# Scratch matmuls in several tilings, and scratch operations on VectorE and Pool, behind the last results of an attention and MLP mix

## The chip, the cores and the metric

The kernel runs on one core of a Trainium2 chip. The metric is the device time of one execution in microseconds; lower is better. The time of the kernel before is the median of two runs on the chip.

The engines are named as the profile names them: PE is TensorE (PEld its weight loads), DVE is VectorE, ACT is ScalarE, POOL is GpSimd, SP is SyncE, which here only issues transfers.

## The reference

From one input `x` (2048 rows of 512) the kernel computes attention with 32 heads that share one key and one value of width 16, computes an MLP with a squared ReLU from another weight set and input, and mixes the two by a gate per row:

```python
g = _sigmoid((x * gate_w).sum(-1, keepdims=True))
a = _A_ref(x, A_wq, A_wk, A_wv, A_wo)      # softmax(q k^T / 4) v, then @ wo
b = _B_ref(x, B_w1, B_b1, B_w2, B_b2)      # relu(x w1 + b1)^2 @ w2 + b2
return g * a + (1 - g) * b
```

All inputs and the output are float32.

## The kernel before, in words

All work is in `mix_kernel`, with an order written out by hand: the program order is the order on every engine's queue, and the tile framework adds only the waits. Attention is cut into 32 steps (`NC * NG`: 4 chunks of 512 rows, 8 groups of 4 heads), each of 16 key tiles in two halves of 256 rows. `scores` (line 723) multiplies 49 augmented rows of queries and keys, two matmuls on the two halves of the array's rows (line 730), and ScalarE takes the exponential of 1024 columns at a time (line 734). `context` (line 737) multiplies the exponentials by the values: plain float32 matmuls of 128 rows by 32 columns, four heads side by side in the array (line 745, `tile_position=(0, h * 32)`).

The projections and the MLP run as a stream of matmuls of 64 rows by 128 columns in float32r, alternating between the two halves of the rows (`stream`, line 188; the matmul is line 214). Operands are split into a rounded part and a rest (`split`, lines 177 to 179), so that three products give the accuracy of float32. `phase` (line 1003) interleaves the two kinds of work, `plan` decides how much of the stream goes between scores, and small jobs for VectorE wait in lists (`chores`, `side`).

The end is what matters here. After the last attention step, `half(acc, 1)` (line 818) transposes, divides and splits the last 256 rows, with a few matmuls on `junk` between (`busy`, line 851) and the flag `bad` computed on VectorE (line 845): 1 if some softmax denominator left the safe range. Then the loop of lines 1068 to 1074 makes the last two output tiles: three full float32r matmuls each (`mm`, line 186), one VectorE operation that gates and adds (line 1073), and a transfer to `out`, the first issued by SP, the second by ACT.

Behind that every engine loads the flag (line 1076) and branches (line 1077): if it is 1, `exact_shift` recomputes the attention; with these inputs it is skipped. The instructions of the closing barrier carry line 1106, where the context ends.

Tiles come from pools with a fixed number of buffers. `at` holds the exponentials as tiles named `e` (128 x 4 x 512, four buffers), `sp` holds the scores as tiles `s` in PSUM (128 x 2 x 512, two buffers), `mp` the stream's PSUM tiles. A tile that takes a used buffer waits for the buffer's last readers.

Of the kernel before, what the change touches and what calls it, by code (L numbers as in the profile page):

```python
# [10 lines left out]
F32 = mybir.dt.float32  # L11
F32R = mybir.dt.float32r
BF = mybir.dt.bfloat16
I32 = mybir.dt.int32
AF = mybir.ActivationFunctionType
OP = mybir.AluOpType
# [6 lines left out]
NC, CH = 4, 512  # L23
# [126 lines left out]
def mix_kernel(ctx: ExitStack, tc: tile.TileContext, xT, wkv, wq, wo, w12, b1, b2, cst, out):  # L150
    nc = tc.nc
# [101 lines left out]
    with fast, tc.tile_pool(name="at", bufs=1) as at, \  # L253
# [790 lines left out]
        while us:  # L1044
            it, k = divmod(us[0], 2 * NK)
# [22 lines left out]
        for j in range(2, 4):  # L1068
# [3 lines left out]
            s = 4 * (NC - 1) + j  # L1072
            nc.vector.scalar_tensor_tensor(ot, po, g[:, s:s + 1], most[0][:, j], op0=OP.mult, op1=OP.add)  # L1073
            (nc.sync, nc.scalar)[j % 2].dma_start(out[s * 128:(s + 1) * 128], ot)

    flag = nc.values_load(bad[0:1, 0:1], min_val=0, max_val=1)
    with tc.If(flag > 0):
        exact_shift(tc, k_aug, v_ext, qs, oTs, gms, ress, cs, wo, split, outproj, stream, unpack)
# [31 lines left out]
```

## Time and profile before

| what | us |
|---|---|
| runs | 1246.99 and 1248.84 |
| median | 1247.91 |
| span of the profiled execution, first to last instruction | 1243.9 |
| PE busy | 1233.2 (99%) |
| ACT busy | 1060.3 (85%) |
| DVE busy | 623.1 (50%) |
| POOL busy | 59.4 (5%) |
| last matmul begins | 1237.33 |
| last VectorE operations begin | 1237.08 |
| last transfer issued | 1238.55 |

The profile is of one execution. The device time of a run holds the span and what lies around it; the median is 4.0 us over the span. In a row of the timeline the first number is the start from the span's start, the second the length, then engine, line, operation, output and inputs, shapes, and how many instructions were merged. In a row of groups the two numbers behind the bar are the busy time in us and the mean of one in ns. In an answer on one line of the code, a row has the operation, its count, and its shortest, median and longest duration in ns, then the first and the last start in us. A matmul of plain float32 leaves two records, one of float32r leaves one; PE's record of a matmul is longer than the distance to the next, since matmuls are pipelined.

### The profile page before, as it was taken

The numbers are of one execution on the slowest core, as the hardware profiler recorded it, in microseconds if no ns is written. First come the engines' busy times: TensorE is split into PE (matmuls) and PEld (weight loads), VectorE is DVE, ScalarE is ACT, GpSimd is POOL, SyncE is SP. The second block draws the span as 40 slices with busy tenths as digits, with TensorE's granted clock in tenths as the row PEclk, the third lists the DMA queues.
The fourth block names the chain that finished last, engine by engine and source line by source line (L and its number), as shares of the span: only waits on it lengthen the run. The fifth ranks groups of instructions, "written<-read, shape, count | busy, mean of one in ns | idle before, by whom it ended". The sixth has DMA issues, their size and how long they took to land.

```text
span 1243.9 us, 24095 instructions
## 1 busy us (share of the span) xinstructions
PE 1233.2 (99%) x9839; PEld 612.5 (49%) x9839; DVE 623.1 (50%) x1246; ACT 1060.3 (85%) x1178; POOL 59.4 (5%) x75
## 2 busy tenths in 40 slices
PE   9999999999999999999999999999999999999997
PEld 4555555555555555555555555555433333343343
DVE  5666665545565542744827365355441454232433
ACT  6888888888888987988988888888899999999985
POOL 1000300000002000000200000002000000000000
PEclk9999999999999999999999999999999999999999
DMA  6334321211232210222202121121110120011101
GB/s 215 101 96 143 105 79 40 82 48 65 69 113 84 75 57 25 82 73 98 72 29 82 65 81 61 56 81 65 56 57 26 35 69 31 31 48 47 44 31 37
DMA packets 44388, 85.57 MB, mean 69 GB/s; under 512 B 10450, under 2 KB 10706, under 8 KB 43760
## 3 DMA queue, kind: packets, MB, share of 16 engines
q1 hardware_dynamic: 37024, 68.27, 17.0%
q0 software_dynamic: 7104, 15.44, 3.7%
q8 instruction: 79, 1.29, 0.4%
q14 instruction: 37, 0.30, 0.1%
q10 hardware_dynamic: 144, 0.26, 0.1%
HBM read 54.68 MB, written 20.97 MB: 61 GB/s over the span
## 4 chain that ended last, share of the span: by engine, by line
PE 96%; ACT 1%; DVE 1%; DMA 0%; issue 0%; SPq 0%; ACTq 0%
PE acc L745 38%; PE mm L214 31%; PE s L730 25%; ACT e L734 1%; PE mm L312 1%; DMA xf<-in_xT 0%; PE mm L186 0%; PE s L322 0%; DVE kmx L334 0%; PE acc L352 0%; ACT w1r L491 0%; PE mm L802 0%; DVE ot L1073 0%; DVE xlagain L179 0%; DVE w1l L487 0%
## 5 line engine op out<-in xcount | busy, mean ns | idle before, releaser
L734 ACT ACTIVATE e<-s 128x1024 f32<-128x1024 f32 x1024 | 980.3, 1023 | 153.5 <-PE s L730 152.0
L745 PE MATMUL acc<-e,v_ext 128*32 128x512 f32 (+1 forms) x4224 | 509.4, 587 | 0.0
L730 PE MATMUL s<-qa,k_aug 49*128 49x512 f32 x2048 | 452.6, 433 | 0.1
L730 PEld LDWEIGHTS s<-qa,k_aug 49*128 49x128 f32 x2048 | 193.7, 183 | 331.8 <-ACT e L734 300.2
L664 DVE SCALAR_TENSOR_TENSOR res<-mm,omg,res 128x512 f32<-128x512 f32 x128 | 95.8, 750 | 252.2 <-PE mm L214 252.2
L214 PE MATMUL mm<-w2r,hr 64*128 64x512 f32 x896 | 212.2, 393 | 1.0 <-DVE big L641 0.6
L745 PEld LDWEIGHTS acc<-e,v_ext 128*32 128x32 f32 x4224 | 102.7, 108 | 208.7 <-issue 202.0
L214 PE MATMUL mm<-w2l,hr 64*128 64x512 f32 x448 | 159.4, 393 | 0.0
L214 PEld LDWEIGHTS mm<-w2r,hr 64*128 64x128 f32 x896 | 129.0, 187 | 18.4 <-DVE res L664 1.2
L214 PEld LDWEIGHTS mm<-w2l,hr 64*128 64x128 f32 x448 | 83.4, 187 | 7.4
L214 PE MATMUL mm<-xragain,w1l 64*128 64x512 f32 x224 | 80.3, 393 | 0.0
L214 PE MATMUL mm<-xr,w1l 64*128 64x512 f32 x224 | 79.4, 393 | 0.0
L214 PE MATMUL mm<-xlagain,w1r 64*128 64x512 f32 x224 | 79.2, 392 | 0.0
L214 PE MATMUL mm<-xragain,w1r 64*128 64x512 f32 x224 | 78.7, 392 | 0.0
L214 PE MATMUL mm<-xl,w1r 64*128 64x512 f32 x224 | 78.5, 391 | 0.0
L214 PE MATMUL mm<-xr,w1r 64*128 64x512 f32 x224 | 77.0, 392 | 0.0
L641 DVE TENSOR_TENSOR big<-big,mm 128x512 f32<-128x512 f32 x56 | 38.5, 687 | 75.0 <-PE mm L214 74.9
L758 DVE RECIPROCAL n<-n 128x86 f32<-128x86 f32 x90 | 61.9, 688 | 3.1
L637 DVE TENSOR_SCALAR big<-mm,b1t 128x512 f32<-128x512 f32 x56 | 42.0, 750 | 39.0 <-PE mm L214 36.9
L214 PEld LDWEIGHTS mm<-xr,w1r 64*128 64x128 f32 x224 | 41.7, 186 | 4.1
L214 PEld LDWEIGHTS mm<-xragain,w1l 64*128 64x128 f32 x224 | 41.7, 186 | 3.9
L214 PEld LDWEIGHTS mm<-xl,w1r 64*128 64x128 f32 x224 | 41.7, 186 | 3.9
(160 smaller groups left out, 1136.8 us busy)
## 6 DMA issues: line engine op xcount, KB each, us to landing
stage<-in_w SPq DMA_DIRECT2D x56, 256.0 KB
qa<-qs SPq DMA_DIRECT2D x186, 64.0 KB
w1f<-in_w SPq DMA_DIRECT2D x28, 256.0 KB
w2f<-in_w SPq DMA_DIRECT2D x28, 256.0 KB
qs<-qr SPq DMA_DIRECT2D x16, 256.0 KB
ress<-res POOLq DMA_DIRECT2D x4, 1024.0 KB, 4.1
qs<-ql POOLq DMA_DIRECT2D x15, 256.0 KB, 8.2
oc<-accs SPq DMA_DIRECT2D x30, 128.0 KB
```

The costliest lines, as they stand in the source:

```text
L214: nc.tensor.matmul(banks[half], a[rows], b[rows], start=i == 0, stop=i == len(terms) - 1)
L312: nc.tensor.matmul(kvq[c][64 * i:64 * i + 64], wkvf[:, k], xf[c, k], start=a == 0, stop=a == 1, skip_group_check=True, tile_position=(0, 6 ...
L637: nc.vector.tensor_scalar(h[0], p, b1t[:, f:f + 1], None, op0=OP.add)
L641: nc.vector.tensor_tensor(h[0], h[0], p, OP.add)
L664: nc.vector.scalar_tensor_tensor(part, p, omg[:, s:s + 1], part, op0=OP.mult, op1=OP.add)
L730: nc.tensor.matmul(s[:, r].rearrange("p (a n) -> p a n", a=2), k_aug[rows, kt * 128:(kt + 1) * 128], qa[it][rows, :, cols], start=True, st ...
L734: nc.scalar.activation(es[u // 2][:, :, mine], s.rearrange("p r (a n) -> p (r a) n", a=2), AF.Exp, scale=SCALE)
L745: nc.tensor.matmul(acc[h * 32:(h + 1) * 32, cols], v_ext[:, kt], es[u // 2][:, h % 2 * 2 + h // 2, mine], start=(kt == 0), stop=(kt == NK ...
L758: nc.vector.reciprocal(n, n)
```

## The change

Behind the loop that makes the last two output tiles, and still inside the pools, the change allocates three tiles `e` and fills them with 0.5 on VectorE, takes two PSUM tiles `s`, and issues matmuls whose results nobody reads. `pairs_of` issues 8 pairs on the two halves of the rows with 128 and then 96 columns; `full` uses the whole array; `half_pairs` and `sub` use tiles of 64 x 128, and of 64 x 32 and 128 x 32 in plain float32. The four loops alternate between tilings. All matmuls have 512 moving columns. After them stand, in program order, operations of 128 x 1024 elements on VectorE (a bit mask, subtractions, copies) and on Pool (copies, subtractions) between the tiles `e`; nobody reads their results either. Output and flag are computed as before. Line numbers below the insertion grow by 60.

```diff
@@ -1073,6 +1073,66 @@
             (nc.sync, nc.scalar)[j % 2].dma_start(out[s * 128:(s + 1) * 128], ot)
 
+        extra = [at.tile([128, 4, CH], F32, name="e", bufs=4) for _ in range(3)]
+        for t in extra:
+            nc.vector.memset(t, 0.5)
+        w, m = [extra[0][:, i].bitcast(F32R) for i in range(2)]
+        wf32, mf32 = [extra[0][:, i] for i in range(2)]
+        two = [sp.tile([128, 2, CH], F32, name="s") for _ in range(2)]
+
+        def sub(n, a, b, rows, cols, dst):
+            for r in range(0, 128, rows):
+                for c in range(0, 128, cols):
+                    k = slice(r, r + rows)
+                    pos = {} if cols == 128 else dict(skip_group_check=True, tile_position=(r, c))
+                    nc.tensor.matmul(dst[c:c + cols, r // rows % 2], a[k, c:c + cols], b[k], start=True, stop=True, **pos)
+
+        def pairs_of(cols):
+            for i in range(8):
+                for r in range(2):
+                    k = slice(64 * r, 64 * r + 64)
+                    nc.tensor.matmul(two[0][:cols, r], w[k, :cols], m[k], start=True, stop=True)
+
+        def full(n):
+            for i in range(n):
+                nc.tensor.matmul(two[1][:, i % 2], w[:, :128], m, start=True, stop=True)
+
+        def half_pairs(n):
+            for i in range(n):
+                sub(i, w, m, 64, 128, two[0])
+
+        pairs_of(128)
+        pairs_of(96)
+        full(8)
+        for i in range(3):
+            half_pairs(3)
+            sub(i, wf32, mf32, 64, 32, two[1])
+            sub(i, wf32, mf32, 64, 32, two[1])
+        for i in range(3):
+            half_pairs(3)
+            sub(i, wf32, mf32, 128, 32, two[1])
+            sub(i, wf32, mf32, 128, 32, two[1])
+        for i in range(3):
+            full(3)
+            sub(i, wf32, mf32, 128, 32, two[0])
+            sub(i, wf32, mf32, 128, 32, two[0])
+        for i in range(3):
+            half_pairs(3)
+            full(3)
+
+        a, b, c2 = extra
+        flat = lambda t, i: t[:, 2 * i:2 * i + 2]
+        ints = lambda t: t.bitcast(I32)
+        for i in range(2):
+            nc.vector.tensor_scalar(ints(flat(b, 0)), ints(flat(a, 0)), -4096, None, op0=OP.bitwise_and)
+            nc.vector.tensor_tensor(flat(b, 1).bitcast(F32R), flat(a, 0), flat(b, 0), OP.subtract)
+            nc.vector.tensor_copy(flat(b, 0).bitcast(F32R), flat(a, 0))
+        for i in range(2):
+            nc.gpsimd.tensor_copy(flat(c2, 0).bitcast(F32R), flat(a, 0))
+            nc.gpsimd.tensor_tensor(flat(c2, 1).bitcast(F32R), flat(a, 0), flat(c2, 0), OP.subtract)
+        for i in range(6):
+            nc.vector.tensor_tensor(flat(b, 1).bitcast(F32R), flat(a, 0), flat(b, 0), OP.subtract)
+
     flag = nc.values_load(bad[0:1, 0:1], min_val=0, max_val=1)
```

## The prediction

> **What bounds the kernel now.** I read the page first: the span, the busy shares, the chain that ended last.
>
> ```profile
> span 1243.9 us, 24095 instructions
> PE 1233.2 (99%) x9839; PEld 612.5 (49%) x9839; DVE 623.1 (50%) x1246; ACT 1060.3 (85%) x1178; POOL 59.4 (5%) x75
> PE 96%; ACT 1%; DVE 1%; DMA 0%; issue 0%; SPq 0%; ACTq 0%
> ```
>
> TensorE is busy 99% of the span and is 96% of the chain, so work appended to its queue has no idle time to hide in. The added code stands behind the last output row on every engine. The instruction order of the two programs differs on PE, DVE and POOL only there; ACT and SP keep their lists. So I take everything up to the last output matmul as unchanged and price only the tail. Its timeline comes next, followed by the instructions at the end of the program, which load the flag `bad`, branch over `exact_shift`, and meet in the closing semaphores.
>
> ```profile
> 1236.41 0.40 PE L186 MATMUL mm<-wol,or 128*128 128x512 f32 x1
> ...
> 1237.33 0.40 PE L186 MATMUL mm<-wor,ol 128*128 128x512 f32 x1
> ...
> 1237.08 1.44 DVE L1073 SCALAR_TENSOR_TENSOR ot<-mm,g,most 128x512 f32<-128x512 f32 x2 [0.73 <-PE mm L186]
> ...
> 1238.55 0.38 ACTq L1074 DMA_DIRECT2D out<-ot  x1
> ```
>
> ```profile
> L1076 POOLq TENSOR_LOAD <-bad x1: 502/502/502, 1235.8 to 1235.8; - x1
> L1076 PEldq TENSOR_LOAD <-bad x1: 482/482/482, 1236.4 to 1236.4; - x1
> ...
> L1077 PEldq COMPARE_BRANCH  x1: 3452/3452/3452, 1237.0 to 1237.0; - x1
> L1077 POOLq INC_SWDGE_SEM  x1: 1272/1272/1272, 1237.2 to 1237.2; - x1
> ...
> L1077 PEldq EVENT_SEMAPHORE  x1: 51/51/51, 1240.5 to 1240.5; - x1
> ...
> L1106 SPq EVENT_SEMAPHORE  x14: 17/28/28, 1241.6 to 1243.9; - x14
> L1106 POOLq EVENT_SEMAPHORE  x4: 17/17/17, 1243.1 to 1243.8; - x4
> L1106 POOLq DRAIN  x3: 46/113/4560, 1238.5 to 1243.6; - x3
> ```
>
> The reader is to see two things. The last matmul ends at 1237.73, the last DVE result at 1238.52, and the program at 1243.9: some 6.2 us follow the last matmul, spent on the output transfer and on closing code. And PE's own branch took 3.45 us, so its closing semaphore came 2.8 us after its last matmul without delaying anybody.
>
> **The change part by part.** Nothing is removed or moved; all of it is added. The program lists 208 new matmuls on PE, 15 operations on DVE and 4 on POOL.
>
> *When PE can start.* The first scratch matmul reads `extra[0]`, which DVE fills behind both L1073 operations. In front of it PE's queue has nothing left; behind it stand only the other scratch matmuls and the closing code. Memset prices:
>
> ```profile
> L297 DVE MEMSET v_ext<- 128x512 f32 x1 | 0.5, 485 | 0.1
> ...
> L259 DVE MEMSET wu<- 128x256 uint32 x1 | 0.3, 272 | 0.9 <-PEq L1102 0.9
> ```
>
> 256 more elements cost 213 ns, so I estimate 485 + 1536 × 0.832 = 1.76 us for 128x2048. The first memset can issue at about 1238.5 and ends at 1240.2; with a semaphore's delay PE starts at 1240.3. The output transfers were issued before and lose nothing.
>
> *What PE's scratch costs.* The steady stage has the tilings wanted, side by side:
>
> ```profile
> 881.38 1.93 PE L745 MATMUL acc<-e,v_ext 128*32 128x512 f32 x16
> 881.83 0.13 PEld L745 LDWEIGHTS acc<-e,v_ext 128*32 128x32 f32 x4 [0.30 <-issue]
> 882.26 0.13 PEld L745 LDWEIGHTS acc<-e,v_ext 128*32 128x32 f32 x4 [0.30 <-issue]
> ...
> 883.23 0.50 PE L730 MATMUL s<-qa,k_aug 49*128 49x512 f32 x2
> ...
> 883.57 0.39 PE L214 MATMUL mm<-xragain,w1r 64*128 64x512 f32 x1
> ...
> 883.57 0.40 PE L214 MATMUL mm<-xragain,w1l 64*128 64x512 f32 x1
> ...
> 883.80 0.39 PE L214 MATMUL mm<-xlagain,w1r 64*128 64x512 f32 x1
> ...
> 884.03 0.41 PE L730 MATMUL s<-qa,k_aug 49*128 49x512 f32 x2
> ...
> 884.37 0.64 PE L745 MATMUL acc<-e,v_ext 128*32 128x512 f32 x4
> ```
>
> Two matmuls on the two halves of the rows start together, and the next pair 0.23 us later (883.57, 883.80, 884.03). The full matmuls of L186 also step by 0.23 us (six of them, 1236.41 to 1237.33 are four steps). Plain f32 with 32 columns (8 matmuls, 16 records) goes in groups of four records, 0.43 us apart (881.83, 882.26); a call of four such matmuls is two groups. From one L745 start to the next are 2.99 us: four groups at 0.43 and four pairs at 0.232 are 2.65 us, so the two changes of tiling cost 0.34 us, 0.17 each.
>
> - Steps at 0.232 us: pairs 8 (128 columns), 8 (96 columns), and 9 in each of three loops; full matmuls 8, and 9 in each of two loops. 43 + 26 = 69 steps, 16.0 us. For the 96-column pairs no row exists; the bounds are the pair step and two steps one after the other (1.9 us more), and I take the pair step, since 49-row pairs run at it too.
> - f32: three loops with six calls of two groups each, 36 groups × 0.43 = 15.5 us. In the first loop the call is 64 rows by 32 columns, eight matmuls on eight places of the array. The trace has no such tiling. Nearest above: both halves one after the other, 6 × 0.86 = 5.2 us more. Nearest below: all eight together, as row halves do in L214 and columns in L745, nothing more. I take the lower one, because both kinds of neighbour run together in the rows above.
> - Changes of tiling: pairs to full and back before the loops 2, the three f32 loops 6 each, the last loop 5, so 25 × 0.17 = 4.3 us. The pair-to-full change is not in the trace; its bounds are 0 and 0.35 us (a record outlasts its step by 0.16 us, and a 64x128 weight load takes 0.19).
>
> Sum 16.0 + 15.5 + 4.3 = 35.8 us; with 0.2 us for the end of the last record PE ends at 1276.3.
>
> The Trainium skill, "TensorEngine Tiling (Array Packing)", Tiling Modes, says that changing the tiling mode drains the TensorE. If the whole drain and the weight load were exposed, the sum would be 25 × (0.35 − 0.17) = 4.5 us larger; the L745 round trip above shows about half of that per change, so I go by the row and keep the other as a rival.
>
> *DVE and POOL beside it.* The nearest rows:
>
> ```profile
> L523 DVE TENSOR_TENSOR xl<-xf,xr 128x1024 fp32r<-128x1024 f32 x4 | 4.9, 1224 | 7.3 <-ACT xr L522 7.3
> ...
> L178 DVE CAST hr<-big 128x512 fp32r<-128x512 f32 x56 | 25.3, 451 | 1.9
> ```
>
> ```profile
> L661 POOL TENSOR_SCALAR res<-big,omg x16: 1555/1574/2247, 147.6 to 855.4; 128x512 f32<-128x512 f32 x16
> ```
>
> DVE: three memsets 5.3, eight subtractions 8 × 1.22 = 9.8, and four single-input operations of 0.7 to 1.2 each, 17.9 to 20 us from 1238.5: done near 1258, some 18 us before PE. POOL begins after the third memset, at 1243.8; at twice L661's 1.57 each, four operations are 12.6 us, done at 1256.4. Its closing path took 7.3 us (from its load at 1235.8 to the end of the long drain at 1243.07), so it reaches the barrier at 1264. Both are covered by PE's tail. Without that cover POOL would end the program at about 1264.5, still 21 us later than now. For a two-input POOL operation no row exists; the bounds are the same price and, at twice the passes and the slowest L661 (2247 ns), three times it.
>
> *The end.* PE must still load the flag (0.48), branch (3.45) and signal, 4.1 us in all. Its sequencer runs ahead of the array (it loaded the flag 1.33 us before the last matmul ended, as soon as the last wait on DVE was over), and no scratch matmul waits on another engine. So the signal comes between 0 and 2.8 us behind the last matmul; I take 1.5. From there the closing waits need 0.8 (POOL's four, 1243.1 to 1243.9) to 2.3 us (all of SP's, from 1241.6); I take 1.4.
>
> End: 1276.3 + 1.5 + 1.4 = 1279.2 against the span's 1243.9, 35.3 us more. The two runs (1246.99 and 1248.84) lie 3.1 and 4.9 us over the profiled span; the median, 1247.91, lies 4.0 over it. That rest I leave unchanged: **1283.2 us**, 2.8% more.
>
> **The rivals.**
> - *The halves of the 64x32 tiling run one after the other.* For it: no row shows eight places at once. Against: halves and columns each run together. 5.2 us more: 1288.4.
> - *A change of tiling exposes drain and weight load.* For it: the two neighbours of the full tiling are never seen back to back. Against: the L745 round trip. 4.5 us more: 1287.7.
> - *PE starts cold.* It idles 2.6 us, from 1237.7 to 1240.3. The granted clock after the last matmul, in the column before the DMA share:
>
> ```profile
> 1237.80:1240.30 2.50, 0.00 (x0) 0.00 (x0) 0.72 (x2) 0.00 (x0) 0.00 (x0) 1.00 0.60 215
> 1240.30:1242.80 2.50, 0.00 (x0) 0.00 (x0) 0.00 (x0) 0.00 (x0) 0.00 (x0) 1.00 0.06 17
> 1242.80:1243.90 1.10, 0.00 (x0) 0.00 (x0) 0.00 (x0) 0.00 (x0) 0.00 (x0) 0.54 0.02 7
> ```
>
> ```profile
> 1.19 3.63 PE L517 MATMUL acc<-wu 128*128 128x512 bf16 x10 [1.19 <-DVE wu L259]
> ```
>
>   The clock held 1.00 for 5 us without a matmul, which speaks against it. The ten cold matmuls at the start took 3.63 us where ten steps of 0.232 are 2.3, so the price is 1.3 us: 1284.5. The Trainium skill, "TensorE: Matmul & The Clock Gate", Part 1, has the clock halve after an idle window of about 3.4 us; the trace agrees in so far as 2.6 us lie within the 5 us that it bore.
> - *POOL ends last.* Its four operations would have to take 6.7 us each instead of 3.1 (1279.2 − 0.85 − 7.3 − 1243.8 = 27.3 us). At that point it ties with PE; each further us per operation adds 4, so 1287 at 7.7 us each. For it: the two-input price and the neighbouring DVE work are unknown. Against: twice is a lot.
> - *Not slower by 2%: f32 is cheaper in the scratch.* Place: the 36 groups. To come under 1272.9 us the sum must lose 10.3 us, so a group would have to cost 0.43 − 10.3 / 36 = 0.14 us or less, a third of the row. At that point it gives 1272.9. For it: no row. Against: the very form, 32 columns of f32 at 512 elements, is in L745.
>
> That the change does not do its work is ruled out by the instruction lists, which hold every scratch operation.
>
> **How the numbers follow.** The forecast has 0.64, the serial halves 0.16, the exposed changes 0.09, the cold start 0.05, POOL last 0.03, cheap f32 0.03. Two per cent is about what a measurement of this kernel tells from no change; all cases but the last exceed it: slower 0.97, same 0.03, faster 0. The range's low end is the forecast without the cost of changes and with the branch fully hidden (1283.2 − 4.3 − 1.5 = 1277.4); its high end takes in the serial halves with the branch exposed by 1.3 us more (1289.7): 1277.4 to 1290.
>
> **What would show it.** In the profile after: the first scratch matmul near 1240.3; L1094 and L1098 steps of 0.23; L1088 f32 groups of 0.43 with eight records together in the first loop; 0.17 at each change; PE's last matmul near 1276; DVE done near 1258 and POOL near 1256; the closing code 2.9 us. It would be wrong if the first f32 loop took about 12 us instead of 7 to 8, if the granted clock fell below 1.00 in the tail, or if POOL's last operation ended after 1271.

## The result, and the profile after

The changed kernel takes 1282.42 us (median; 1282.36 to 1282.49) against 1247.91 us, a ratio of 1.0276 with a 95% interval of 1.0256 to 1.0295: slower, at 1283.2 forecast. The profiled execution took 1282.36 us. Its page opens like this; the last line is the chain that ended last, by line:

```profile
span 1280.2 us, 24723 instructions
...
PE 1271.6 (99%) x10143; PEld 629.0 (49%) x10143; DVE 646.0 (50%) x1261; ACT 1060.0 (83%) x1178; POOL 67.9 (5%) x79
...
PE acc L745 37%; PE mm L214 31%; PE s L730 24%; PE s L1088 2%; ACT e L734 1%; PE s L1098 1%; PE mm L312 1%; PE s L1094 0%; DMA xf<-in_xT 0%; PE mm L186 0%; PE s L322 0%; DVE kmx L334 0%; DVE e L1078 0%; PE acc L352 0%; ACT w1r L491 0%
```

PE gained 38.4 us of busy time and the span 36.3. The scratch lines L1088, L1098 and L1094 stand in the chain, and of the other scratch operations only one DVE fill, L1078. The end of the timeline (start, duration, engine, line, and in brackets the idle time before it):

```profile
1237.10 0.40 PE L186 MATMUL mm<-wor,ol 128*128 128x512 f32 x1
...
1238.66 1.76 DVE L1078 MEMSET e<- 128x2048 f32 x1 [0.38 <-issue]
...
1240.48 5.53 PE L1094 MATMUL s<-e 64*128 64x512 f32 x32 [2.99 <-DVE e L1078]
1240.80 1.76 DVE L1078 MEMSET e<- 128x2048 f32 x1 [0.38 <-issue]
...
1245.94 2.11 PE L1098 MATMUL s<-e 128*128 128x512 f32 x8
1246.23 3.24 POOL L1132 TENSOR_TENSOR e<-e 128x1024 fp32r<-128x1024 f32 x1
1247.26 2.76 DVE L1129 CAST e<-e 128x1024 fp32r<-128x1024 f32 x1
...
1248.87 0.18 PEld L1088 LDWEIGHTS s<-e 64*32 64x32 f32 x16 [0.37 <-issue]
1249.33 0.15 PEld L1088 LDWEIGHTS s<-e 64*32 64x32 f32 x8 [0.28 <-issue]
...
1249.76 0.15 PEld L1088 LDWEIGHTS s<-e 64*32 64x32 f32 x8 [0.28 <-issue]
...
1251.50 3.28 DVE L1128 TENSOR_TENSOR e<-e 128x1024 fp32r<-128x1024 f32 x1
...
1255.54 7.52 DVE L1134 TENSOR_TENSOR e<-e 128x1024 fp32r<-128x1024 f32 x6
...
1277.26 0.96 PE L1098 MATMUL s<-e 128*128 128x512 f32 x3
```

The last output matmul starts at 1237.10, as before within 0.23 us, so all the time was lost behind it. PE waits 2.99 us for the first fill, then works from 1240.48 to 1278.22. DVE is done at 1263.06, 15 us ahead. In the first f32 loop eight weight records go together, 0.43 us apart (1249.33, 1249.76).

But 16 pairs of L1094 took from 1240.48 to 1245.94, which is 5.46 us where sixteen steps of 0.232 and a change of tiling are 3.9. The windows tell why (the first figures are PE's busy time and count; the granted clock is the one ahead of the DMA share):

```profile
1237.38:1240.79 3.41, 0.42 (x3) 0.30 (x4) 2.67 (x3) 0.00 (x0) 0.00 (x0) 1.00 0.44 159
1240.79:1244.20 3.41, 3.41 (x18) 2.60 (x16) 3.02 (x2) 0.00 (x0) 0.00 (x0) 0.50 0.00 0
1244.20:1247.60 3.40, 3.40 (x23) 2.36 (x20) 3.33 (x4) 0.00 (x0) 2.63 (x2) 1.00 0.02 5
```

For 3.41 us the clock was halved: the cold start, the rival to which I had given 0.05, took place, and a granted clock below 1.00 in the tail was one of the prediction's own signs of being wrong. The closing code:

```profile
L1136 PEldq TENSOR_LOAD <-bad x1: 490/490/490, 1274.6 to 1274.6; - x1
...
L1137 PEldq COMPARE_BRANCH  x1: 3855/3855/3855, 1275.2 to 1275.2; - x1
...
L1137 PEldq EVENT_SEMAPHORE  x1: 51/51/51, 1279.1 to 1279.1; - x1
...
L1166 POOLq EVENT_SEMAPHORE  x4: 17/17/17, 1279.4 to 1280.1; - x4
```

PE's sequencer loaded the flag 3.6 us ahead of the last matmul's end, so most of its 3.86 us branch is covered; the signal comes 0.9 us behind the last matmul, and the span ends 1.1 us later.

### The profile page after: what moved, and what is told of

It is laid out like the page before. It is cut to its first block, busy times and chain, and to the rows that moved or that the text cites. A ratio compares the mean times of both kernels' runs of the same rounds, so it can differ in the third digit from the quotient of the medians.

```text
span 1280.2 us, 24723 instructions
## 1 busy us (share of the span) xinstructions
PE 1271.6 (99%) x10143; PEld 629.0 (49%) x10143; DVE 646.0 (50%) x1261; ACT 1060.0 (83%) x1178; POOL 67.9 (5%) x79
## 4 chain that ended last, share of the span: by engine, by line
PE 97%; ACT 1%; DVE 1%; DMA 0%; issue 0%; SPq 0%; ACTq 0%
PE acc L745 37%; PE mm L214 31%; PE s L730 24%; PE s L1088 2%; ACT e L734 1%; PE s L1098 1%; PE mm L312 1%; PE s L1094 0%; DMA xf<-in_xT 0%; PE mm L186 0%; PE s L322 0%; DVE kmx L334 0%; DVE e L1078 0%; PE acc L352 0%; ACT w1r L491 0%
## 5 line engine op out<-in xcount | busy, mean ns | idle before, releaser
L214 PE MATMUL mm<-w2r,hr 64*128 64x512 f32 x896 | 211.9, 392 | 1.0 <-DVE big L641 0.6
L214 PE MATMUL mm<-w2l,hr 64*128 64x512 f32 x448 | 159.6, 393 | 0.0
L214 PEld LDWEIGHTS mm<-w2r,hr 64*128 64x128 f32 x896 | 129.1, 187 | 18.3 <-DVE res L664 1.2
L214 PEld LDWEIGHTS mm<-w2l,hr 64*128 64x128 f32 x448 | 83.4, 186 | 7.6
L214 PE MATMUL mm<-xragain,w1l 64*128 64x512 f32 x224 | 80.2, 393 | 0.0
L214 PE MATMUL mm<-xr,w1l 64*128 64x512 f32 x224 | 79.5, 393 | 0.0
L214 PE MATMUL mm<-xlagain,w1r 64*128 64x512 f32 x224 | 79.3, 392 | 0.0
L214 PE MATMUL mm<-xragain,w1r 64*128 64x512 f32 x224 | 78.8, 392 | 0.0
L214 PE MATMUL mm<-xl,w1r 64*128 64x512 f32 x224 | 78.7, 391 | 0.0
L214 PE MATMUL mm<-xr,w1r 64*128 64x512 f32 x224 | 76.8, 392 | 0.0
L641 DVE TENSOR_TENSOR big<-big,mm 128x512 f32<-128x512 f32 x56 | 38.4, 686 | 75.8 <-PE mm L214 75.7
L214 PEld LDWEIGHTS mm<-xl,w1r 64*128 64x128 f32 x224 | 41.8, 186 | 4.0
L214 PEld LDWEIGHTS mm<-xlagain,w1r 64*128 64x128 f32 x224 | 41.8, 187 | 3.9
L214 PEld LDWEIGHTS mm<-xr,w1r 64*128 64x128 f32 x224 | 41.7, 186 | 3.9
```

The costliest lines, as they stand in the source:

```text
L214: nc.tensor.matmul(banks[half], a[rows], b[rows], start=i == 0, stop=i == len(terms) - 1)
L641: nc.vector.tensor_tensor(h[0], h[0], p, OP.add)
```

## The experiments

In the expectations A is the explanation that I held after the result: PE alone sets the end, by the sum of the prediction plus one stretch of halved clock; the other letters are its rivals. Single medians hide a difference of a few us, since the runs of the kernel before are themselves spread over 3.7 us (last section). So beside each time I use two distances inside the profile: from the start of the last output matmul to the start of the last scratch matmul ("tail"), and from the first to the last scratch start ("scratch"). In the changed kernel these are 40.72 and 37.34 us. Each kernel below is the changed one with the edit shown, save the last two, which edit the kernel before.

**pe_alone** leaves out the scratch operations on DVE and POOL (the three fills stay).

```diff
-        a, b, c2 = extra
...
-            nc.gpsimd.tensor_copy(flat(c2, 0).bitcast(F32R), flat(a, 0))
...
-            nc.vector.tensor_tensor(flat(b, 1).bitcast(F32R), flat(a, 0), flat(b, 0), OP.subtract)
```

> The scratch operations on VectorE and Pool are left out; the three fills and all scratch matmuls stay. Theory A, the chain of scratch matmuls behind the last results sets the end and the other engines' scratch lies beside it: no change from the changed kernel, 1282.4 us within 0.7, last matmul ending near 1278. Rival B, the scratch on VectorE and Pool slows the matmuls through SBUF or delays the closing code: 1 to 4 us less, 1278 to 1281.

Measured: 1283.32 us (1281.89 to 1283.78), ratio 1.029 [1.0272, 1.0307]. Tail 40.60, scratch 37.22. Nothing came back, so DVE and POOL carry none of the loss. The median is 0.9 us over the changed kernel's, slightly more than I had allowed; the profile has a second halved stretch, from 30.25 us, far ahead of the end.

**vector_alone** leaves out all the scratch matmuls.

```diff
-        pairs_of(128)
...
-            half_pairs(3)
-            full(3)
```

> All scratch matmuls are left out; the fills and the scratch on VectorE and Pool stay. Theory A: now VectorE's queue, which ended at 1263.1 in the changed kernel, sets the end: the span ends near 1264.3, and the time is 1266.5 to 1268.3, some 15 us below the changed kernel and 19 over the kernel before. Rival B, Pool's closing path (its long drain ended at 1258.3) decides: span near 1259.2. Rival C, the fills, copies and subtractions were slow because matmuls read the same tile at the time: VectorE then ends near 1258 and the span near 1259.5.

Measured: 1268.94 us (1267.37 to 1269.93), ratio 1.0175 [1.0158, 1.0192]. The last output matmul and the last DVE operations of its timeline:

```profile
1240.20 0.40 PE L186 MATMUL mm<-wor,ol 128*128 128x512 f32 x1
...
1258.55 7.52 DVE L1115 TENSOR_TENSOR e<-e 128x1024 fp32r<-128x1024 f32 x6
```

DVE ends 25.87 us behind the last output matmul's start; in the changed kernel it is 25.97. So the matmuls do not slow DVE. Without PE's cover the program ends at 1267.2, 27.0 us behind that matmul: DVE, not POOL, is next in line. The time lies over my 1266.5 to 1268.3, since in this profile two halved windows ahead of the end put the last output matmul at 1240.20, 3.1 us later than in the changed kernel.

**ready** lets the scratch matmuls read `k_aug`, which was filled long before, so that they need not wait for a fill.

```diff
-        w, m = [extra[0][:, i].bitcast(F32R) for i in range(2)]
-        wf32, mf32 = [extra[0][:, i] for i in range(2)]
+        w, m = [k_aug[:, i * CH:(i + 1) * CH] for i in range(2)]
+        wf32, mf32 = [k_aug[:, i * CH:(i + 1) * CH].bitcast(F32) for i in range(2)]
```

> The scratch matmuls read the key tile, filled long before, in place of the tile filled behind the last results; counts and tilings are the same. Theory A, the wait for the fill costs 3.1 us and the idle time that it makes costs 1.7 us more because the clock halves for one window: matmuls go on without a gap at full clock, 1277.6 us (4.8 less). Rival B, the first 8 pairs were slow for another reason than the idle time (the tiling, the fresh tile): 1279.3 and pairs still 0.43 apart at the start. Rival C, the start of PE does not matter since something else ends the program: 1282.4.

Measured: 1278.01 us (1277.54 to 1279.27), ratio 1.0252 [1.0235, 1.0269]. Its timeline, then two windows:

```profile
1237.53 0.40 PE L186 MATMUL mm<-wor,ol 128*128 128x512 f32 x1
...
1237.85 3.99 PE L1094 MATMUL s<-k_aug 64*128 64x512 f32 x32
```

```profile
1237.85:1241.26 3.41, 3.41 (x31) 2.83 (x32) 2.66 (x4) 0.00 (x0) 0.00 (x0) 1.00 0.45 163
1241.26:1274.00 32.74, 32.74 (x278) 12.78 (x274) 21.45 (x14) 0.00 (x0) 8.57 (x4) 1.00 0.01 2
```

The 32 records now take 3.99 us instead of 5.53, the clock stays at 1.00, and the gap is gone. The tail falls from 40.72 to 36.14 us: 3.05 by the gap, 1.5 by the clock. Scratch is 35.82, and 36.05 with the last step, against the prediction's 35.8.

**bridge** keeps the fill but gives PE 13 bf16 matmuls on old data while it waits. This separates the two parts of ready.

```diff
+        fill = mp.tile([128, CH], F32, name="mm")
+        for _ in range(13):
+            nc.tensor.matmul(fill, cs[:, :64].bitcast(BF), cs[:, :CH // 2].bitcast(BF), start=True, stop=True)
         pairs_of(128)
```

> 13 bf16 matmuls of 0.215 us on a tile that is ready (2.8 us) fill PE's wait for the first fill; the rest is as in the changed kernel. Theory A: the scratch matmuls begin at the same time, near 1240.4, but at full clock, so 1280.7 us, 1.7 less, though PE does more work. Rival B, the slow first pairs have another cause: 1282.4 and pairs 0.43 apart. Rival C, the clock halves regardless of the work in the window because bf16 matmuls of one tile count for little: 1282.4 with a granted clock below 1 after 1240.

Measured: 1281.42 us (1280.44 to 1282.55), ratio 1.0281 [1.0264, 1.0298], in its interval no different from the changed kernel, where I had expected 1280.7. So the medians do not decide this one; the profiled timeline does:

```profile
1237.44 2.98 PE L1106 MATMUL mm<-cs 128*128 128x512 bf16 x13
...
1240.58 3.98 PE L1094 MATMUL s<-e 64*128 64x512 f32 x32 [0.16 <-DVE e L1078]
```

PE does more and the wait for the fill ends at the same place, but the pairs run in 3.98 us, and the distance from first to last scratch start is 35.79 us instead of 37.34. The halved stretch cost 1.5 us, and it was the idling that made room for it: all five profiles in which PE idles until the fill is done have it (the changed kernel's first, again, pe_alone, sorted, half_rows), and the two in which PE has work instead, ready and bridge, have none.

**sorted** does the same matmuls sorted by tiling: 3 changes instead of 25.

```diff
-        full(8)
-        for i in range(3):
-            half_pairs(3)
...
+        for i in range(9):
+            half_pairs(3)
+        full(26)
+        for i in range(6):
+            sub(i, wf32, mf32, 64, 32, two[1])
+        for i in range(6):
+            sub(i, wf32, mf32, 128, 32, two[1])
+        for i in range(6):
+            sub(i, wf32, mf32, 128, 32, two[0])
```

> The same scratch matmuls, but sorted by tiling: all pairs, all full ones, all of 64x32, all of 128x32; 3 changes of tiling in place of 25. Theory A, each change costs 0.17 us: 22 fewer changes save 3.7 us, so the stretch from the last output matmul to the last scratch matmul shrinks from 40.7 us in the changed kernel to 37.0, and the time is near 1278.9. Rival B, the extra at the ends of groups belongs to the f32 groups and not to the changes of tiling: the stretch stays at 40.7 within 0.5. Rival C, a change exposes the whole drain and weight load, 0.35 each: 7.7 us less, 33.0.

Measured: 1279.28 us (1277.82 to 1280.27), ratio 1.026 [1.0244, 1.0276]. Sorted, each price can be read straight from the timeline:

```profile
1240.76 5.55 PE L1094 MATMUL s<-e 64*128 64x512 f32 x32 [2.98 <-DVE e L1078]
...
1246.14 6.32 PE L1088 MATMUL s<-e 64*128 64x512 f32 x54
...
1252.39 6.21 PE L1098 MATMUL s<-e 128*128 128x512 f32 x26
...
1258.54 15.82 PE L1088 MATMUL s<-e 64*32 64x512 f32 x192
```

27 pairs from 1246.14 to 1252.39 are 0.231 us each, 26 full matmuls to 1258.54 are 0.237 (each stretch with one change in it), and the 36 f32 groups behind them are 15.8 us with a change and the end of the last record. The halved stretch is there as before (5.55). Tail is 36.38, where I had expected 37.0. Scratch falls from 37.34 to 33.00 us (37.21 in the second profile of the changed kernel), so 22 changes cost 4.2 to 4.3 us: 0.19 each, where I had 0.17 and the exposed drain of the rival would be 0.35.

**half_rows** lets the 64x32 calls use the upper 64 rows alone: 24 of the 96 f32 matmuls are left out.

```diff
-        def sub(n, a, b, rows, cols, dst):
-            for r in range(0, 128, rows):
+        def sub(n, a, b, rows, cols, dst, upto=128):
+            for r in range(0, upto, rows):
...
-            sub(i, wf32, mf32, 64, 32, two[1])
-            sub(i, wf32, mf32, 64, 32, two[1])
+            sub(i, wf32, mf32, 64, 32, two[1], 64)
+            sub(i, wf32, mf32, 64, 32, two[1], 64)
```

> In the first f32 loop only the upper 64 rows are multiplied: 4 matmuls of 64x32 a call in place of 8, so 24 of the 96 f32 matmuls are left out. Theory A, the eight run at the same time: nothing changes, the stretch from the last output matmul to the last scratch matmul stays at 40.7 us within 0.5 (if the clock halves as before). Rival B, the two halves of the rows share the array's time: 2.6 to 5.2 us less.

Measured: 1282.20 us (1281.81 to 1285.39), ratio 1.0292 [1.0274, 1.031]. Scratch is 37.04 us, 0.30 less. Its windows explain most of that:

```profile
1236.46:1239.87 3.41, 0.92 (x4) 0.40 (x3) 2.77 (x3) 0.00 (x0) 0.00 (x0) 1.00 0.41 154
1239.87:1243.28 3.41, 2.92 (x14) 2.35 (x16) 2.66 (x3) 0.00 (x0) 0.00 (x0) 0.50 0.02 5
```

The halved stretch began 0.49 us ahead of the first scratch matmul, so only 2.92 us of it fell on work, worth some 0.24 us. Half of the small matmuls gone changed nothing else, where one half behind the other would have given back 5.2: the eight run together.

**dve_alone** leaves out the scratch matmuls and POOL's scratch operations.

```diff
-            nc.gpsimd.tensor_copy(flat(c2, 0).bitcast(F32R), flat(a, 0))
-            nc.gpsimd.tensor_tensor(flat(c2, 1).bitcast(F32R), flat(a, 0), flat(c2, 0), OP.subtract)
```

> All scratch matmuls and Pool's scratch are left out; the fills and VectorE's scratch stay. Theory A, Pool's operations slow VectorE's next to them by sharing its way to SBUF: without them subtractions take 1.22, copies 0.69 and the mask 0.63 us, and VectorE ends 21 us behind the start of the last output matmul in place of 25.9, so the span is about 5 us below that of the run with both. Rival B, VectorE's long ones (1.9 to 3.3 us) have their own cause, such as reading and writing one tile: they stay, and so does the end.

Measured: 1262.28 us (1261.6 to 1262.97), ratio 1.0124 [1.0105, 1.0143]. DVE's operations:

```profile
1245.64 1.23 DVE L1109 TENSOR_TENSOR e<-e 128x1024 fp32r<-128x1024 f32 x1
1246.90 0.69 DVE L1110 CAST e<-e 128x1024 fp32r<-128x1024 f32 x1
...
1250.34 7.52 DVE L1112 TENSOR_TENSOR e<-e 128x1024 fp32r<-128x1024 f32 x6
```

The subtraction that took 3.28 us beside POOL takes 1.23, the copy 0.69 instead of 2.76, and DVE ends 20.4 us behind the last output matmul instead of 25.9. POOL's operations slow DVE's; PE's do not. The rows of the changed kernel fit a DVE operation that waits until POOL's has ended and then runs at its own length: the copy from 1247.26 ends 0.55 us behind POOL's subtraction (1246.23 and 3.24), the subtraction from 1251.50 ends 1.09 us behind POOL's of 1250.99 (2.70 long). No run separates this from two operations that share the way at a lower rate.

**again** is the changed kernel once more, unedited, for another profile of it.

> The changed kernel once more. Theory A, the clock halves for one window of about 3.4 us because the wait for the fill leaves most of such a window idle; where the window lies differs from run to run, so the halved stretch begins at another distance from the last output matmul (3.7 us in the first profile, 3.1 without the other engines' scratch), and costs 1.2 to 1.7 us; the median is 1282.4 within 1. Rival B, the halving was chance: no halved stretch, 1.7 us less.

Measured: 1283.72 us (1281.16 to 1284.86), ratio 1.0288 [1.0272, 1.0305]. Tail 40.60, scratch 37.21, and a halved stretch:

```profile
1242.44:1245.86 3.42, 3.16 (x15) 2.50 (x17) 2.67 (x3) 0.00 (x0) 0.00 (x0) 0.50 0.01 2
```

It begins 3.12 us behind the last output matmul's start (1239.32), in the first profile 3.69: in these two profiles the cost is the same, the place is not. The median is 1.3 us over the first, outside the "within 1" that I had allowed; this profile has a further halved stretch, from 30.71 us. And the halving is not in every run. Of the five, two have a mean clock of 1.000, which leaves no room for a stretch of 3.41 us (0.9987), and spans of 1279.0 and 1279.2 us; the other three have 0.996 to 0.997 and 1281.6 to 1282.7. The second run of the result has 1.000 as well, but a span of 1280.3; no trace of it was kept, so what filled its time is open.

**woven** and **woven2** try to make the kernel before faster. Several profiles had halved stretches near 25 to 40 us, behind a long row of short matmuls (L352, 17 columns). The kernels put pieces of the projection (L214) between the rows of tiles, so that PE is never lightly used for 3.4 us. Woven does it at one place; woven2 also at an earlier one, with the weights that it needs fetched earlier.

```diff
-        v_tiles(range(9, 16), vp)
+        for i in range(9, 16):
+            v_tiles([i], vp)
+            if next(lazy, None):
+                left -= 1
```

> The kernel before, without any scratch work. The runs of the kernel before spread over 1245.6 to 1248.8, and three profiles in which the last output matmul comes 1.3 to 3 us later have a granted clock of 0.5 for one or two windows near 25 to 35 us, each behind a stretch of matmuls with 17 columns. Here one product of the stream stands behind each of the seven value matmuls of line 1040, so that PE has full-width work there. Theory A, the sparse stretch is what halves the clock: no halved window after 28 us in the profile, a narrower spread, and a median 0.5 to 1.5 us below the kernel before. Rival B, the sparse stretch is harmless and the spread has another cause: the spread and the median stay as they are, within 0.5.

Measured: 1251.33 us (1249.76 to 1255.1), ratio 1.0045 [1.0032, 1.0059]: some 0.45% slower, where I had expected 0.5 to 1.5 us less. The timelines of woven, then of the kernel before, at that place:

```profile
28.04 0.50 PE L730 MATMUL s<-qa,k_aug 49*128 49x512 f32 x2
28.47 0.40 PE L352 MATMUL acc<-cs,kvc 128*128 128x17 f32 x2
28.80 0.49 PE L214 MATMUL mm<-xr,wql 64*128 64x512 f32 x1
...
29.22 0.40 PE L352 MATMUL acc<-cs,kvc 128*128 128x17 f32 x2
...
33.66 0.39 PE L730 MATMUL s<-qa,k_aug 49*128 49x512 f32 x2
```

```profile
27.76 0.50 PE L730 MATMUL s<-qa,k_aug 49*128 49x512 f32 x2
28.19 1.74 PE L352 MATMUL acc<-cs,kvc 128*128 128x17 f32 x14
29.86 0.50 PE L730 MATMUL s<-qa,k_aug 49*128 49x512 f32 x2
```

One round, 28.47 to 29.22, takes 0.75 us where its short matmuls (1.67 us for seven of them) and one pair step are 0.47: two changes of tiling a round, again. The stretch grows from 2.10 to 5.62 us and holds seven pair steps that have been moved there, 1.6 us. The profile has no halved window ahead of the end, as expected, but the six runs spread over 5.3 us with mean clocks of 0.993 to 0.999: the spread did not shrink.

> As the run with seven products woven in, and six products of the stream also take the place of the six fillers between the earlier value matmuls (line 584, moved behind the setup of the stream; the rounding of one query weight is moved two phases up). Theory A: no halved window at all between 20 and 40 us, runs within 1 us of each other and a median 1 to 2.5 us below the kernel before. Rival B: spread and median unchanged within 0.5. Rival C, the fillers were what kept the clock up, and products that wait for their operands leave PE idle: slower than the kernel before by 1 us or more.

Measured: 1253.26 us (1250.54 to 1253.64), ratio 1.0043 [1.003, 1.0056]. Its profile has four halved windows, two in each of 25.87 to 32.69 and 36.11 to 42.93. Neither version beats the kernel before.

## Why the prediction was right, and where its terms were off

- *All the loss is behind the last output.* Right: the last output matmul starts 0.23 us earlier than before, and ready, which changes the tile that the scratch reads and so when it can start, gives back 4.4 us.
- *PE starts at 1240.3.* From L186's last start 2.97 us were forecast, 3.38 measured (in six profiles). The fill itself is 1.76 us, as estimated; mis-sized was its start, which I had back to back with L1073: the row shows 0.38 us of idle time ahead of it, and as much ahead of the two fills behind, so a fill holds DVE's queue for 2.14 us.
- *35.8 us of scratch.* At full clock right: 36.05 in ready. Steps of 0.231 to 0.237, groups of 0.43, 96-column pairs at the pair step (32 records in 3.99 us), eight matmuls together (the first f32 loop took 8.3 us in the changed kernel, from 1247.98 to 1256.29; 12 would have been the sign of serial halves). The change of tiling was 0.19 instead of 0.17. Neither the serial halves nor the fully exposed drain took place. The Trainium skill, "TensorEngine Tiling (Array Packing)", Tiling Modes, says that a change of mode drains the array; the trace agrees in that each change costs time, about half of the 0.35 us that I had reckoned for the whole drain and the weight load.
- *The clock stays at 1.00.* This step failed, and 1.5 us stand in its place (I had 1.3 as the price of the rival). My argument was that in the kernel before the clock held 1.00 for 5 us behind the last matmul. Cut where the clock changes and one stretch of 3.41 us ahead of that, the same profile reads otherwise:

```profile
1236.07:1239.48 3.41, 1.66 (x8) 1.02 (x6) 1.72 (x3) 0.00 (x0) 0.00 (x0) 1.00 0.24 85
1239.48:1242.90 3.42, 0.00 (x0) 0.00 (x0) 0.00 (x0) 0.00 (x0) 0.00 (x0) 1.00 0.25 88
1242.90:1243.92 1.02, 0.00 (x0) 0.00 (x0) 0.00 (x0) 0.00 (x0) 0.00 (x0) 0.50 0.02 8
```

  The first 1.8 us behind the last matmul share their window with 1.66 us of PE work, the next window is empty, and with its end the clock is halved. So the row told where the windows lay in that one execution and no more: halved stretches of 3.41 us began at 1239.87, 1240.79, 1241.54, 1241.98 and 1242.44 in five profiles, at other distances from the last matmul, each behind a window with 0.42 to 0.92 us of PE work. By these rows a wait of 3 us halves the clock when most of it falls into one window. That would also explain the two runs of again without a halved stretch, but no trace of them was kept. Where between 0.92 and 1.66 us of work the border lies, the rows do not show. The Trainium skill, "TensorE: Matmul & The Clock Gate", Part 1, says that the window runs freely and does not start with the kernel; the trace agrees (3.41 us, another place in each of these profiles), and I should have taken that sentence against my row. Its other condition, an idle window, is stricter than these rows: PE was busy 0.42 us of the window ahead of the halving, in half_rows 0.92.
- *The end costs 2.9 us.* It was 1.98: the sequencer ran 3.6 us ahead, not 1.3, so the branch was exposed by 0.9 instead of 1.5 us.
- *4.0 us lie outside the span.* Mis-sized: they are 2.1 to 2.2 in the runs of the changed kernel. In 27 runs of the kernel before they are 1.7 to 1.9; by that the two runs that I was shown had longer spans than the profiled execution. The 1.8 us that I took too much there hid the 1.0 us that the span had too little (+0.4 by the start, +1.7 by the scratch, −0.9 by the end, −0.2 by the last output). That 1283.2 came out within 0.8 us is therefore luck in part: two errors in opposite directions. Against the time that the profiled execution of the kernel before would have by its span, 1243.9 + 1.8 = 1245.7 (an estimate), the change cost 36.7 us, not 34.5.
- *DVE near 1258, POOL near 1256.* DVE was done at 1263.06. Alone it takes what I had summed (20.4 us behind the last output matmul; 20.7 forecast); the rest is POOL. The Trainium skill, "GPSIMD Engine Reference", section 1, has the two engines share their SBUF interfaces, with contention for DVE operations that have two SBUF inputs or run in a 2-port mode; the trace agrees for the subtraction, which has two inputs, and the copy became longer too, though no run shows in which mode it ran. POOL's four operations took 8.6 us, not 12.6, and were done at 1253.7. (In the rival on POOL, 27.3 us among four operations are 6.8 us each, not 6.7.) Both lay under PE's tail, so neither cost anything.

## What to carry to other kernels

Work put behind the last result on an engine that is already 99% busy costs its full serial length, so price it from the steps of the steady stage, and add 0.2 us for each change of tiling, which sorting by tiling saves. Do not let PE wait some 3 us ahead of a burst: the wait can count twice, once itself and once as a stretch of halved clock behind it (here 3.0 and 1.5 us), and one profile in which the clock held is no promise for the next run. Compare a time with the span of the same execution: what lay outside the span hardly varied here (1.7 to 1.9 us in the kernel before), while the spans varied by 3.6.

## What the runs showed of the hardware

*The clock is halved ahead of the end too, and the runs spread with it.* In vector_alone there are halved windows well ahead of the end:

```profile
21.95:25.36 3.41, 3.20 (x30) 2.59 (x30) 2.79 (x7) 2.52 (x5) 0.00 (x0) 1.00 0.23 47
25.36:28.78 3.42, 3.42 (x16) 2.73 (x15) 1.96 (x4) 2.05 (x2) 0.00 (x0) 0.50 0.38 132
```

In the first of them PE has a record on 3.20 of 3.41 us, but part of these are short matmuls; in the next the clock is 0.50. Ahead of the halved stretches at 30.71 (again) and 30.25 (pe_alone) a record of PE covers all of the 3.41 us. So the share of time with a record does not tell when the clock is halved. The 27 runs of the kernel before fall into three groups, by time, span and the mean granted clock:

| runs | time, us | span, us | mean clock |
|---|---|---|---|
| 11 | 1245.2 to 1246.1 | 1243.4 to 1244.3 | 0.998 to 1.000 |
| 11 | 1247.0 to 1247.5 | 1245.3 to 1245.6 | 0.997 to 0.998 |
| 5 | 1248.3 to 1248.8 | 1246.5 to 1247.0 | 0.996 |

One halved window lowers the mean clock by 0.5 × 3.41 / 1244 = 0.0014 and costs some 1.5 us, about one row of the table. The profiles fit: the last output matmul starts at 1237.0 to 1237.5 in those without such a window after the first 7 us, at 1238.83 and 1239.32 with one, at 1240.20 with two. Time and mean clock go together, though not strictly: 0.998 stands in two rows, probably because the mean also counts halved time behind the last matmul, which costs nothing (in the profile of the kernel before from 1242.90). That the short matmuls are the cause stays open: the two woven kernels, made to test it, changed too much else.

*DVE's large fills do not follow each other closely:* three of 1.76 us start 2.14 apart, with 0.38 us that the profile puts down to issue. Whether that is idle time or a part of the fill that its record leaves out, no run shows.

*What lies outside the span grows with scratch operations on DVE or POOL:* 2.1 to 2.2 us with both, 1.8 to 1.9 without them in pe_alone, 1.7 to 1.9 in the kernel before. In dve_alone, without the matmuls and POOL's operations, it is 2.5 to 2.6, in vector_alone 2.4 to 2.7. Why is open.
